# Issuing eight small w_phi loads between two transposed weight loads, on the sync queue of a TensorE-bound kernel

## The chip, the core and the metric

One Trainium2 chip, one of its cores. The metric is the device time of one execution in microseconds (us); lower is better.

## The reference

Two blocks read the same input `x` (1 x 2048 x 512, bf16) and are mixed by a sigmoid gate. Block A is linear attention with a feature map: each of 32 heads multiplies its 16-wide query and key by its own 16 x 16 matrix `w_phi` before two softmaxes. Block B is a gMLP with a 2048 x 2048 spatial matrix `w_sp`.

```python
qkv = (x @ wqkv).reshape(B, S, 3, 32, 16) ...           # q, k, v
pq  = einsum('bhsd,hdf->bhsf', q, w_phi)                # the same w_phi for q and k
pk  = einsum('bhsd,hdf->bhsf', k, w_phi)
phi = concat([softmax(p), softmax(-p)])                 # for q and for k
... kv, z, num / den, @ wo                              # a
z   = gelu(x @ w_in);  z2 = layernorm(z[..., 688:])
b   = (z[..., :688] * (w_sp @ z2 + b_sp)) @ w_out
out = g * a + (1 - g) * b                               # g = sigmoid(x . gate_w)
```

## The kernel before

Since `q @ w_phi` is `x @ (W_q @ w_phi)`, the kernel folds `w_phi` into the query and key weights once: `fold(1)` (the key fold) and `fold(0)` (the query fold). Each is 64 small matmuls that read a transposed copy of the weight (`wqkT`) and a block-diagonal copy of `w_phi` (`wphi`). Filling that copy takes eight small loads, one for each place of a head within a block of 128 rows.

All these loads are issued by the sync engine (SP), in program order, from one queue:

```python
    nc.sync.dma_start(out=brow[0:NT, :], in_=B_b_sp.rearrange("(t p) -> t p", p=P))
    for qk in (1, 0):                                   # key, then query, transposed
        nc.sync.dma_start_transpose(
            out=wqkT[:, qk * NDT:(qk + 1) * NDT, :], in_=A_wqkv[:, qk * D:(qk + 1) * D])
    heads = A_w_phi.rearrange("(kc u) e f -> u e kc f", u=8)
    for u in range(8):                                  # the eight small loads
        us = slice(u * DH, (u + 1) * DH)
        nc.sync.dma_start(out=wphi[us, :, us], in_=heads[u])
    for h in range(2):
        nc.sync.dma_start(out=wv_sb[:, 2 * h:2 * h + 2, :], in_=...)      # w_v
    for q in range(NCH):                                # four slabs of w_sp, transposed
        nc.sync.dma_start_transpose(
            out=wspT[:, :, q * CH:(q + 1) * CH], in_=B_w_sp[q * CH:(q + 1) * CH, :])
```

The program fixes the order of TensorE's instructions (in before's trace the folds come at 26.00 and 36.04 us). The folds stand in the middle of the first stage, behind the second z2 tile of the third and fourth block of rows:

```python
        for c in range(NCH):
            ts = list(range(c * 4, c * 4 + 4))
            for tt in ts:
                if c > 0:
                    z2_tile(tt)                         # 8 matmuls on line 191
                if c >= 2 and tt % 4 == 1:
                    later = fold(3 - c)                 # c=2: key, c=3: query; line 307
            ...                                         # z1 tiles, layernorm
```

A load is thus late only if it lands after TensorE has worked through the matmuls ahead of its fold.

The softmax here doesn't subtract the row's maximum and nothing guards it: scores larger than these inputs give would overflow.

Of the kernel before, what the change touches and what calls it, by code (L numbers as in the profile page):

```python
# [18 lines left out]
DH = 16  # L19
# [16 lines left out]
def kernel(  # L36
# [14 lines left out]
    nc = tc.nc  # L51
# [20 lines left out]
    wphi = early.tile([P, NDT, P], BF16, name="wphi")  # L72
# [32 lines left out]
        out=ramp[:, 0, :], data0=ones32[:, :], data1=zeros[:, :], initial=0.0,  # L105
# [4 lines left out]
    for q in range(4):  # L110
        qs = slice(32 * q, 32 * q + 32)
        nc.vector.tensor_tensor(
            out=ident[qs, qs], in0=ramp[qs, 0, :], in1=ramp[qs, 1, :], op=ALU.is_equal)
    nc.gpsimd.memset(brow[:], 0.0)
    nc.gpsimd.memset(wphi[:], 0.0)
    def load_z2w(eng, dt):
# [11 lines left out]
        out=scrap[:, :], in_=nc.const_aps.tensor(1.0, [P, 1], BF16), func=AF.Gelu_apprx_tanh)  # L128
# [5 lines left out]
    for h in range(2):  # L134
        nc.sync.dma_start(
            out=w_z1[:, 2 * h:2 * h + 2, :], in_=w_in_v[:, 2 * h:2 * h + 2, 0:FH])
    for i in range(4, 8):
        x_dma_T(i)
    for q in range(2, NCH):
        nc.sync.dma_start_transpose(  # L140
            out=xT[:, :, q * CH:(q + 1) * CH], in_=x2[q * CH:(q + 1) * CH, :]
        )
    nc.sync.dma_start(out=brow[0:NT, :], in_=B_b_sp.rearrange("(t p) -> t p", p=P))
    for qk in (1, 0):
        nc.sync.dma_start_transpose(
            out=wqkT[:, qk * NDT:(qk + 1) * NDT, :], in_=A_wqkv[:, qk * D:(qk + 1) * D])
    heads = A_w_phi.rearrange("(kc u) e f -> u e kc f", u=8)
    for u in range(8):
        us = slice(u * DH, (u + 1) * DH)
        nc.sync.dma_start(out=wphi[us, :, us], in_=heads[u])  # L150
    for h in range(2):
        nc.sync.dma_start(
            out=wv_sb[:, 2 * h:2 * h + 2, :],
            in_=A_wqkv[h * 2 * P:(h + 1) * 2 * P, 2 * D:3 * D].rearrange("(dt p) n -> p dt n", p=P),
        )
    for q in range(NCH):
        nc.sync.dma_start_transpose(
            out=wspT[:, :, q * CH:(q + 1) * CH], in_=B_w_sp[q * CH:(q + 1) * CH, :]
# [4 lines left out]
        out=mask4[:], in_=mask4[:], pattern=[[-32, NG]],  # L163
# [3 lines left out]
        out=mask4[:], in_=mask4[:], pattern=[[32, NG]],  # L167
# [3 lines left out]
        out=mask64[:, :, :], in_=mask4[:, :, None].to_broadcast([P, NG, DH]))  # L171
# [472 lines left out]
```

## Time and profile before

| | before |
|---|---|
| time, median of the first 3 runs | 206.76 us (206.36 to 206.82) |
| span in the profile | 204.5 us |
| TensorE busy | 200.8 us (98%) |
| granted TensorE clock (share of full speed), mean | 1.000 |
| key fold's operands read from | 25.9 us |
| query fold's operands read from | 36.0 us |

The page of before: the span; busy time, share of the span and instruction count of each engine (PE is TensorE); and the chain of waits, by engine and by line.

```profile
span 204.5 us, 3996 instructions
...
PE 200.8 (98%) x1557; PEld 119.9 (59%) x1557; DVE 130.4 (64%) x283; ACT 74.8 (37%) x122; POOL 45.6 (22%) x76
...
PE 98%; DVE 0%; issue 0%
PE mm L454 37%; PE zp L191 18%; PE mm L355 14%; PE mm L515 9%; PE mm L509 7%; PE mm L395 7%; PE kvacc L411 2%; PE at L467 2%; PE zp L222 1%; PE mm L520 1%; PE zp L307 0%; PE pq L280 0%; PE at L478 0%; PE pq L307 0%; DVE ob L527 0%; PE zp L230 0%
```

TensorE's own list of waits (what it waited for: us in all, times, longest):

```profile
engine line waited for: us in total, times, longest us
PE zp L222 <- PEq L628: 0.8, 1, 0.8
```

98% of the chain that ended last is TensorE, and TensorE waits for nothing after its first matmul. Line 191 is the first stage, line 454 the spatial matmul. A change that only moves loads can save at most what TensorE waits for loads, and here that list has no load in it.

The timeline of the SP queue (start, us, what was issued, out<-in, count). Durations are the time that SP spent issuing, not the transfer (the two transposes below took 2.43 and 2.30 us to issue and landed 5.2 to 5.5 us after their start):

```profile
15.37 4.78 SPq L145 DMA_TRANSPOSE wqkT<-in_A_wqkv_dram  x2
20.25 4.13 SPq L150 DMA_DIRECT2D wphi<-in_A_w_phi_dram  x8
24.43 0.94 SPq L152 DMA_DIRECT2D wv_sb<-in_A_wqkv_dram  x2
25.41 36.83 SPq L157 DMA_TRANSPOSE wspT<-in_B_w_sp_dram  x4
```

The key and query transposes take 4.78 us to issue together, the eight w_phi loads 4.13 us. The last w_phi load is issued at about 24.0 us (0.42 us ahead of the end of its row) and lands 1.6 us later at the earliest: at about 25.6.

The instructions of line 307, the folds. The first row gives the semaphore events of the weight loader's queue, the rest the loader's idle time by cause:

```profile
L307 PEldq EVENT_SEMAPHORE  x2: 51/51/51, 24.5 to 25.6; - x2
its engine sat idle before it (us, times) until:
  issue: 0.6, 2
```

The chain from 22 to 38 us (start, us, what; the many rows of 0.02 us inside the folds are left out):

```profile
23.64 2.36 PE zp L191 x16
26.00 0.12 PE zp L307 x2
...
26.58 9.45 PE zp L191 x64
36.04 0.12 PE zp L307 x2
...
36.75 1.27 PE zp L191 x8
```

The matmuls ahead of the key fold end at 26.00 us. The fold takes until 26.58 (0.58 us), 64 matmuls of line 191 until 36.04, the query fold until 36.75 (0.71 us). The second event, at 25.6, is the last w_phi load. So w_phi came 0.4 us ahead of its use: close, but in time.

### The profile page before, as it was taken

How to read it: one execution, taken by the hardware profiler on the slowest of the kernel's cores; microseconds unless marked ns; L12 is line 12 of the kernel's file. 1: busy time of each engine (PE TensorE's matmuls, PEld its weight loads, DVE VectorE, ACT ScalarE, POOL GpSimd, SP SyncE). 2: the span in 40 equal slices, each digit the busy share in tenths (PEclk: the TensorE clock that was granted, in tenths of full speed). 3: DMA queues.
4: the chain of work that ended last, by engine and by line, in shares of the span. 5: the costliest groups of instructions: out<-in, count | busy, mean ns of one | idle time of the engine just before them, and what ended most of it. 6: DMA issues, size and time to landing. Idle time of an engine off the chain costs nothing.

```text
span 204.5 us, 3996 instructions
## 1 busy us (share of the span) xinstructions
PE 200.8 (98%) x1557; PEld 119.9 (59%) x1557; DVE 130.4 (64%) x283; ACT 74.8 (37%) x122; POOL 45.6 (22%) x76
## 2 busy tenths in 40 slices
PE   8999999999999999999999999999999999999994
PEld 4666666655665555656565666555555555665642
DVE  4567484837977587979797789555566645633332
ACT  3566678796222333332424042222251136002303
POOL 3020202021523325334242442222204220200000
PEclk9999999999999999999999999999999999999999
DMA  6999699999999027940423219853567458552833
GB/s 194 252 205 171 80 151 290 146 278 247 256 249 213 3 38 182 287 94 16 75 48 45 51 38 120 154 109 64 105 161 80 90 113 183 63 96 51 156 64 104
DMA packets 89931, 27.22 MB, mean 133 GB/s; under 512 B 84184, under 2 KB 89912, under 8 KB 89912
## 3 DMA queue, kind: packets, MB, share of 16 engines
q1 hardware_dynamic: 87744, 24.99, 65.4%
q10 hardware_dynamic: 2168, 1.98, 3.5%
q8 instruction: 12, 0.20, 0.4%
q14 instruction: 7, 0.06, 0.1%
HBM read 4.15 MB, written 2.10 MB: 31 GB/s over the span
## 4 chain that ended last, share of the span: by engine, by line
PE 98%; DVE 0%; issue 0%
PE mm L454 37%; PE zp L191 18%; PE mm L355 14%; PE mm L515 9%; PE mm L509 7%; PE mm L395 7%; PE kvacc L411 2%; PE at L467 2%; PE zp L222 1%; PE mm L520 1%; PE zp L307 0%; PE pq L280 0%; PE at L478 0%; PE pq L307 0%; DVE ob L527 0%; PE zp L230 0%
## 5 line engine op out<-in xcount | busy, mean ns | idle before, releaser
L454 PE MATMUL mm<-z2all,wspT 128*128 128x344 bf16 x512 | 79.9, 309 | 0.0
L454 PEld LDWEIGHTS <-wspT 128*128 128x128 bf16 x512 | 49.0, 98 | 25.3
L191 PE MATMUL zp<-w_z,xT 128*128 128x344 bf16 (+1 forms) x254 | 38.1, 310 | 0.0
L359 ACT ACTIVATE eq<-mm 128x512 bf16<-128x512 f32 x32 | 17.4, 594 | 51.4 <-PE mm L355 25.7
L363 DVE TENSOR_REDUCE zs<-eq 128x64 f32<-128x1024 bf16 x16 | 19.5, 1220 | 20.0 <-ACT eq L359 20.0
L191 PEld LDWEIGHTS <-xT 128*128 128x128 bf16 x254 | 24.4, 98 | 11.8
L359 ACT ACTIVATE ek<-mm 128x512 bf16<-128x512 f32 x32 | 17.3, 600 | 27.1 <-PE mm L355 27.1
L459 DVE SCALAR_TENSOR_TENSOR ucat<-mm,bT,z1all 128x344 bf16<-128x344 f32 x32 | 17.4, 544 | 15.0 <-PE mm L454 15.0
L372 POOL TENSOR_TENSOR eq<-eq,ratio 128x512 bf16<-128x512 bf16 x16 | 16.9, 1055 | 44.6 <-DVE ratio L371 36.7
L531 ACT ACTIVATE ob<-mm,g_inv 128x512 bf16<-128x512 f32 (+1 forms) x15 | 10.1, 680 | 33.1 <-PE mm L520 28.5
L363 DVE TENSOR_REDUCE zs<-ek 128x64 f32<-128x1024 bf16 x16 | 19.3, 1209 | 2.8 <-ACT ek L359 2.8
L515 PE MATMUL mm<-wspT,uT 128*128 128x512 bf16 (+2 forms) x85 | 20.1, 367 | 0.0
L355 PEld LDWEIGHTS <-xT 128*128 128x128 bf16 x128 | 12.2, 98 | 12.0
L372 POOL TENSOR_TENSOR ek<-ek,ratio 128x512 bf16<-128x512 bf16 x16 | 16.9, 1056 | 2.2 <-DVE ratio L371 1.7
L509 PE MATMUL mm<-wspT,oT 128*128 128x512 bf16 (+2 forms) x68 | 16.6, 366 | 0.0
L355 PE MATMUL mm<-wq_p,xT 128*128 128x512 bf16 x64 | 16.4, 379 | 0.0
L395 PE MATMUL mm<-wv_sb,xT 128*128 128x512 bf16 x64 | 16.4, 379 | 0.0
L355 PE MATMUL mm<-wk_p,xT 128*128 128x512 bf16 x64 | 16.3, 379 | 0.0
L209 DVE BATCH_NORM_STATS2 bn<-z2all 128x6 f32<-128x344 bf16 x32 | 14.9, 501 | 0.0
L206 ACT ACTIVATE z2all<-zp 128x688 bf16<-128x688 f32 x16 | 11.8, 744 | 7.3 <-PE zp L191 7.2
L260 ACT ACTIVATE z1all<-zp 128x688 bf16<-128x688 f32 x16 | 11.9, 744 | 5.1 <-PE zp L191 4.6
L515 PEld LDWEIGHTS <-uT 128*128 128x128 bf16 x85 | 8.1, 98 | 9.4 <-issue 0.2
(77 smaller groups left out, 142.7 us busy)
## 6 DMA issues: line engine op xcount, KB each, us to landing
out_dram<-ob ACTq DMA_DIRECT2D x12, 128.0 KB, 2.4
wspT<-in_B_w_out_dram SPq DMA_DIRECT2D x2, 640.0 KB, 4.9
w_z<-in_B_w_in_dram SPq DMA_DIRECT2D x2, 344.0 KB, 4.7
w_z<-in_B_w_in_dram SPq DMA_DIRECT2D x3, 172.0 KB, 3.5
wv_sb<-in_A_wqkv_dram SPq DMA_DIRECT2D x2, 256.0 KB, 2.7
wspT<-in_A_wo_dram SPq DMA_DIRECT2D x2, 256.0 KB, 4.0
out_dram<-ob SPq DMA_DIRECT2D x3, 128.0 KB, 1.8
uT<-ucat SPq DMA_TRANSPOSE x16, 2.8
```

Of the source, the lines that this page charges most:

```text
L191: nc.tensor.matmul(zp[:, j, 0:n], lhsT=xT[:, dt, tt * P:(tt + 1) * P], rhs=wt[:, dt, j * HF:j * HF + n], start=(dt == 0), stop=(dt == NDT ...
L209: nc.vector.bn_stats(out=bn6[:, tt, j, :], in_=z2v[:, j, :])
L260: nc.scalar.activation(out=z1all[:, tt, :].rearrange("p (j n) -> p j n", j=2), in_=zp[:, :, 0:HF], func=AF.Gelu_apprx_tanh,)
L355: nc.tensor.matmul(ps[:, :], lhsT=xT[:, dt, tt * P:(tt + 1) * P], rhs=w[:, dt, :], start=(dt == 0), stop=(dt == NDT - 1))
L359: nc.scalar.activation(out=e[:, :, a, :], in_=ps[:, :].rearrange("p (h f) -> p h f", f=DH), func=AF.Exp, scale=1.0 - 2.0 * a)
L363: nc.vector.tensor_reduce(out=z[:].rearrange("p h a -> p (h a)"), in_=e[:].rearrange("p h a f -> p (h a) f"), axis=AX.X, op=ALU.add,)
L372: nc.gpsimd.tensor_tensor(out=e[:, :, 1, :], in0=e[:, :, 1, :], in1=ratio[:, :, None].to_broadcast([P, H, DH]), op=ALU.mult)
L395: nc.tensor.matmul(v_ps[:, :], lhsT=xT[:, dt, tt * P:(tt + 1) * P], rhs=wv_sb[:, dt, :], start=(dt == 0), stop=(dt == NDT - 1))
L454: nc.tensor.matmul(gp[:, 0:HF], lhsT=wspT[:, st, tt * P:(tt + 1) * P], rhs=z2all[:, st, j * HF:(j + 1) * HF], start=(st == 0), stop=(st == ...
L459: nc.vector.scalar_tensor_tensor(out=ucat[tt % NU][:, c0 + j * HF:c0 + (j + 1) * HF], in0=gp[:, 0:HF], scalar=bT[:, tt:tt + 1], in1=z1all[ ...
L509: nc.tensor.matmul(acc, lhsT=oTs[tt][:, g, :], rhs=wo_t[:, g, c0:c1], start=start and g == 0, stop=stop and g == NG - 1)
L515: nc.tensor.matmul(acc, lhsT=uTs[tt][:, i + ft, :], rhs=w_main[i][:, ft, c0:c1], start=start and ft == 0, stop=False)
```

## The change

The intent is to have w_phi in place early. The key fold needs it together with the key weights, ten microseconds before anything needs the query weights, yet it is issued behind the query transpose. The change swaps the two.

```diff
+    heads = A_w_phi.rearrange("(kc u) e f -> u e kc f", u=8)
     for qk in (1, 0):
         nc.sync.dma_start_transpose(
             out=wqkT[:, qk * NDT:(qk + 1) * NDT, :], in_=A_wqkv[:, qk * D:(qk + 1) * D])
-    heads = A_w_phi.rearrange("(kc u) e f -> u e kc f", u=8)
-    for u in range(8):
-        us = slice(u * DH, (u + 1) * DH)
-        nc.sync.dma_start(out=wphi[us, :, us], in_=heads[u])
+        for u in range(8 if qk == 1 else 0):
+            us = slice(u * DH, (u + 1) * DH)
+            nc.sync.dma_start(out=wphi[us, :, us], in_=heads[u])
```

The order of instructions on TensorE, VectorE, ScalarE and GpSimd is the same in both kernels; only SP's order changes, and with it some semaphore numbers.

## The prediction

> **What bounds the kernel now.** TensorE. On the page PE is busy 200.8 of 204.5 us (98%), the chain of waits is 98% PE, and PE's waits total 0.8 us, before the first matmul. The granted clock is 1.000. In the table by stretches PE is busy for the whole of each stretch from 15 to 75 us. So a load can cost time if it comes late, but can hardly give any back.
>
> **What the change does.** The same DMAs on the same SP queue; the order of instructions on PE, DVE, ACT and POOL is unchanged. Only the queue's order from 15 to 25 us moves. In before's timeline of SP:
> - key transpose issued 15.4 to 17.8 us, query transpose 17.85 to 20.15 (5.2 to 5.5 us from issue to landing);
> - eight w_phi loads 20.25 to 24.4 us (0.42 us each, 0.75 for one; landing after 1.6 to 3.3 us), the last issued at 24.0, so landing at about 25.6;
> - w_v from 24.4, four w_sp transposes from 25.4.
>
> PE reads w_phi and the key weights in the key fold at 25.9 us; the query fold is at 36.0; w_v is read at 45.6; w_sp at 46.3.
>
> So the last w_phi load lands only about 0.3 us ahead of the key fold: its semaphore event on the weight loader is at 25.6 us, and the weight loader idles 0.28 us. That is what the change aims at: w_phi 2.4 us earlier. But the matmuls queued ahead run until 26.0, so PE itself does not stand still; and the query fold, whose operands landed long before, starts with about the same weight-loader idle and the same 0.12 us step in the chain. That idle belongs to the fold's start, not to the load. Gain on the critical path: 0 to 0.15 us.
>
> **What it costs.** The query transpose is issued about 4.2 us later, at about 22, and should land at about 27.3, 8.7 us before its fold. The lane waits move too (a load waits for the DMA eight before it): the last w_phi load now waits for the key transpose, landed at about 20.7, when it is due at about 21.5; the query transpose waits for the first w_phi load. Neither should hold the queue by over 0.5 us. w_v should start within 0.5 us of 24.4, w_sp of 25.4; the first w_sp slab lands 12.9 us later, at 38.3, 8 us before its use. All this is slack. [...]I expect no new serialisation from alternating them.
>
> **Prediction.** 206.7 us, 80% range 206.1 to 207.3 (before: 206.36 to 206.82). Faster by over 2%: 0.01; within 2%: 0.98; slower by over 2%: 0.01.
>
> **What would show each step.** Right: PE busy about 200.8 and span about 204.5; key fold at 25.9 and query fold at 36.0, within 0.1 us; last w_phi issue at about 21.6, landing before 24; query transpose issued at about 22, landing by 28; w_sp from 25 to 26 us; the 0.28 us of weight-loader idle still there. Wrong: that idle gone and the fold earlier (the load was the wait); any PE wait at the query fold; w_sp over 1 us later.
>
> **What would make it wrong.** Unprofiled executions in which w_phi comes late, a cost that the profile hides (gain up to 1 us); a transpose that waits for all earlier plain loads, pushing the query transpose past 36 us; a shift of the later transposes of u and q on the same queue.

What is left of that sentence is my expectation alone ("them" are transposes and plain loads).

## The result, and the profile after

| | before | after |
|---|---|---|
| median of 6 runs | 206.66 us (206.23 to 206.82) | 206.22 us (206.05 to 206.73) |
| ratio, 95% interval | | 0.9987 (0.9971 to 1.0002) |
| span in the profile | 204.5 us | 204.5 us |
| TensorE busy | 200.8 us | 200.6 us |
| last w_phi issued | 24.0 us | 21.3 us |
| query transpose issued | 17.85 us | 21.79 us |

A ratio is the mean time of one kernel's runs over that of the other's of the same rounds, so it is not quite the ratio of the medians quoted. Executions over 1.5% slower than the fastest of the same kernel are left out of the means. The result is the same within 2%, and the interval includes one.

The page of after:

```profile
span 204.5 us, 3996 instructions
...
PE 200.6 (98%) x1557; PEld 119.5 (58%) x1557; DVE 130.5 (64%) x283; ACT 74.6 (36%) x122; POOL 45.8 (22%) x76
...
PE 95%; DMA 2%; SPq 1%; DVE 0%; issue 0%
```

TensorE's waits in after:

```profile
PE zp L222 <- PEq L628: 0.8, 1, 0.8
PE zp L191 <- DMA xT<-in_A_x_dram: 0.3, 1, 0.3
```

The 2% of DMA in the chain and the new 0.3 us wait belong to the first transposed load of `x`, at 7 us, long before the moved loads: the chain is followed back through that wait, so the matmuls ahead of it no longer count. The change cannot have caused it, and the profile of the same text run again (below) has no such wait.

The SP queue in after:

```profile
15.33 2.51 SPq L146 DMA_TRANSPOSE wqkT<-in_A_wqkv_dram  x1
17.94 3.81 SPq L150 DMA_DIRECT2D wphi<-in_A_w_phi_dram  x8
21.79 1.30 SPq L146 DMA_TRANSPOSE wqkT<-in_A_wqkv_dram  x1
23.14 1.22 SPq L152 DMA_DIRECT2D wv_sb<-in_A_wqkv_dram  x2
24.40 37.03 SPq L157 DMA_TRANSPOSE wspT<-in_B_w_sp_dram  x4
```

The eight w_phi loads begin at 17.94 us instead of 20.25, and the query transpose comes 3.9 us later. Something else was not foreseen: this transpose took 1.30 us to issue instead of 2.30, so that w_v and w_sp are issued about a microsecond *earlier* than before (24.40 against 25.41 us for w_sp).

The folds in after, and the chain of the same stretch:

```profile
L307 PEldq EVENT_SEMAPHORE  x2: 51/51/51, 24.6 to 24.8; - x2
...
  issue: 0.6, 2
```

```profile
23.81 2.36 PE zp L191 x16
26.16 0.12 PE zp L307 x2
...
26.75 9.45 PE zp L191 x64
36.20 0.12 PE zp L307 x2
...
36.79 1.28 PE zp L191 x8
```

The key fold takes 0.59 us and its start still has the same 0.28 us of loader idle (0.6 us over the two folds): that idle was never the load's. TensorE starts the fold 0.16 us later than in before; the wait at 7 us lies on that path. But the query fold takes 0.59 us here instead of 0.71, so that at the first matmul behind it, 36.79 against 36.75 us, most of the difference is gone. From that matmul to the copy of the last output tile (201.72 us in before, 201.76 in after) both profiles take 164.97 us, to the hundredth.

### The profile page after: what moved, and what is told of

Its sections match the earlier page's. It is cut to its first block, busy times and chain, and to the rows that moved or that the text cites. A ratio compares the mean times of both kernels' runs of the same rounds, so it can differ in the third digit from the quotient of the medians.

```text
span 204.5 us, 3996 instructions
## 1 busy us (share of the span) xinstructions
PE 200.6 (98%) x1557; PEld 119.5 (58%) x1557; DVE 130.5 (64%) x283; ACT 74.6 (36%) x122; POOL 45.8 (22%) x76
## 4 chain that ended last, share of the span: by engine, by line
PE 95%; DMA 2%; SPq 1%; DVE 0%; issue 0%
PE mm L454 37%; PE zp L191 17%; PE mm L355 14%; PE mm L515 8%; PE mm L509 7%; PE mm L395 7%; DMA xT<-in_A_x_dram 2%; PE kvacc L411 2%; PE at L467 2%; PE mm L520 1%; SPq L117 1%; PE zp L307 0%; PE at L478 0%; SPq L119 0%; PE pq L307 0%; DVE ob L527 0%
## 5 line engine op out<-in xcount | busy, mean ns | idle before, releaser
L454 PEld LDWEIGHTS <-wspT 128*128 128x128 bf16 x512 | 49.0, 98 | 25.3
L191 PEld LDWEIGHTS <-xT 128*128 128x128 bf16 x254 | 24.3, 98 | 12.4 <-DMA xT<-in_A_x_dram 0.6
```

What stands on the lines that cost most here:

```text
L191: nc.tensor.matmul(zp[:, j, 0:n], lhsT=xT[:, dt, tt * P:(tt + 1) * P], rhs=wt[:, dt, j * HF:j * HF + n], start=(dt == 0), stop=(dt == NDT ...
L454: nc.tensor.matmul(gp[:, 0:HF], lhsT=wspT[:, st, tt * P:(tt + 1) * P], rhs=z2all[:, st, j * HF:(j + 1) * HF], start=(st == 0), stop=(st == ...
```

## The experiments

**Two theories.** Mine: w_phi is in time in the old order, or so nearly that only tenths can be won, and the 0.4 us between the medians is spread. The rival: in executions that the one profile does not show, w_phi came late, and the new order saves it. Out of the chain views comes a measure far finer than the times: *the stretch*, from the end of the matmuls ahead of the key fold to the first matmul behind the query fold. It is free of what happens at the start and after the folds. The table has all 13 profiles. (The experiments ran on two chips; each ratio is to runs of before in the same rounds, on the same chip.) "Event" is the last of the weight loader's semaphore events at the key fold, "ready" the end of the matmuls ahead of it, "behind" the first matmul behind the query fold, and "rest" goes from there to the copy of the last output tile.

| profile | event | ready | behind | stretch | rest | span |
|---|---|---|---|---|---|---|
| *old order* | | | | | | |
| before | 25.6 | 26.00 | 36.75 | 10.75 | 164.97 | 204.5 |
| same_text | 26.1 | 25.92 | 36.96 | 11.04 | 164.97 | 204.7 |
| before_again | 25.4 | 26.74 | 37.37 | 10.63 | 164.97 | 205.1 |
| pad_2 | 26.1 | 26.31 | 36.93 | 10.62 | 164.98 | 204.8 |
| pad_4 | 26.8 | 26.50 | 37.60 | 11.10 | 164.97 | 205.6 |
| *w_phi earlier* | | | | | | |
| after | 24.8 | 26.16 | 36.79 | 10.63 | 164.97 | 204.5 |
| after_again | 24.7 | 26.05 | 36.68 | 10.63 | 164.97 | 204.4 |
| after_third | 25.3 | 26.73 | 37.36 | 10.63 | 164.97 | 205.1 |
| after_x_earlier | 25.3 | 26.71 | 37.34 | 10.63 | 164.97 | 205.1 |
| wphi_first | 25.1 | 26.50 | 37.12 | 10.62 | 164.97 | 204.9 |
| *w_phi or query later* | | | | | | |
| wphi_after_wv | 25.9 | 26.82 | 37.44 | 10.62 | 164.98 | 205.2 |
| query_after_slab | 25.3 | 26.71 | 37.88 | 11.17 | 164.97 | 205.6 |
| wphi_after_slab | 35.9 | 26.09 | 49.02 | 22.93 | 164.97 | 216.8 |

Where w_phi is early, the event comes 1.4 us ahead of "ready": that is merely when the loader's queue gets there. Where the gap is smaller, the load set it.

### The old text and the new text again, five rounds each

Edit of the first: none, the text of before. Edit of the second: none, the text of after.

> The kernel before, unchanged: a measure of what a ratio near one is worth. All theories: ratio 1.000, within 0.2%. If it comes out as far from one as the changed kernel's 0.9987, that 0.9987 is no sign of a gain.

> The changed kernel again, against before in 5 rounds on this chip. My theory (w_phi was never waited for by TensorE; the 0.4 us between the two medians is spread): ratio 0.999 to 1.001, spans overlapping those of before, TensorE's wait list without w_phi. Rival (executions in which w_phi came late cost the old order a few tenths): 0.998 to 0.999 again, with an interval below one. In either case w_sp should again start about 1 us earlier than before (24.4 against 25.4 us).

| | median | before beside it | ratio | 95% interval |
|---|---|---|---|---|
| same_text | 206.32 us | 206.41 us | 0.9990 | 0.9976 to 1.0004 |
| after_again | 206.21 us | 206.41 us | 0.9992 | 0.9976 to 1.0007 |

The unchanged text came out 0.9990 of itself. So neither 0.9987 nor 0.9992 is a sign of a gain, or against one: five rounds do not resolve 0.2 us. In the new text's profile w_phi is not among TensorE's waits. That alone proves little: the list of same_text has the same single row, `PE zp L222 <- PEq L628: 0.8, 1, 0.8`, and yet w_phi was late there, as shown next. In the new text w_sp was issued at 25.18 us, earlier than in the profile of same_text beside it (25.88), but not at the 24.4 us that I wrote.

The profile of same_text, however, goes against the strict form of my theory. Its queue, its folds and its chain:

```profile
15.40 5.46 SPq L145 DMA_TRANSPOSE wqkT<-in_A_wqkv_dram  x2
20.96 3.89 SPq L150 DMA_DIRECT2D wphi<-in_A_w_phi_dram  x8
```

```profile
L307 PEldq EVENT_SEMAPHORE  x2: 51/51/51, 24.4 to 26.1; - x2
...
  issue: 0.5, 2
  DMA wphi<-in_A_w_phi_dram: 0.3, 1
```

```profile
23.56 2.35 PE zp L191 x16
25.92 0.12 PE zp L307 x2
...
26.04 0.12 issue
...
26.79 9.45 PE zp L191 x64
36.24 0.12 PE zp L307 x2
...
36.96 1.13 PE zp L191 x7
```

Here the two transposes took 5.46 us to issue instead of 4.78, the last w_phi event came at 26.1 us, and TensorE was ready at 25.92. The key fold took 0.87 us (25.92 to 26.79) instead of 0.58. The loader's row for w_phi is no proof by itself, being as long as the 0.28 us of idle before every fold. But the trace has the fold stopping after its first matmuls and going on at 26.16 us, 0.13 us after the last w_phi load landed at 26.03; in pad_4 and wphi_after_slab (below), where w_phi was made late, that lag is 0.14 us. The wait that the change was meant to remove exists: 0.28 us, in this one execution of the unchanged text.

### A third profile of each

> A third profile of before's text, for the stretch from the end of the matmuls ahead of the key fold to the first matmul after the query fold. It was 10.75 and 11.04 us in the two profiles of that text, and 10.62 to 10.63 us in the four profiles whose w_phi was in time. My theory: the last w_phi event comes between 25.0 and 26.2 us, depending on how long the two weight transposes took to issue (4.1 to 5.5 us so far), and the stretch is 10.62 us where it comes ahead of 25.9 and up to 0.4 us longer where not. Rival (the order itself adds a fixed cost to the folds): at least 0.12 us longer whatever the landing time.

> A third profile of the changed text. Both theories: stretch 10.62 to 10.63 us, last w_phi landed over 2 us ahead of the key fold, the stretch from there to the last output store equal to the other profiles' 164.97 us. Any other value of the last would mean that the change reaches stages after the folds.

Edits: none. One execution each, 206.82 us both (state unknown, as with every single run). The old text's queue this time:

```profile
15.39 4.44 SPq L145 DMA_TRANSPOSE wqkT<-in_A_wqkv_dram  x2
19.92 4.05 SPq L150 DMA_DIRECT2D wphi<-in_A_w_phi_dram  x8
```

4.44 us of issue, event at 25.4, ready at 26.74, stretch 10.63 us: no loss at all. The fixed cost that the rival of this run expected is ruled out, and the new text gave 10.63 us for the third time. The mean of the three old profiles is (10.75 + 11.04 + 10.63) / 3 = 10.81 us, 0.18 us above the new text's 10.63: 0.09% of the time, well within all intervals above. Only about half of it can be put down to the order: of these three profiles one has lost time at the key fold (0.28 us, in the mean 0.09). The rest is 0.12 us in before and 0.13 in same_text, in the query fold (0.71 and 0.72 instead of 0.59 us), whose operands had long landed. The trace has it as one pause of 0.13 us between two of the fold's last matmuls (36.44 to 36.57 us in before). The three other profiles that the table calls old order (before_again, pad_2, pad_4) lack it. Its cause stays open.

### w_phi first of all

> The eight w_phi loads ahead of both weight transposes: w_phi even earlier (issued from about 15.4 to 19.2 us), both transposes about 3.8 us later, the key weights landing at about 24 us, ahead of the key fold at 26. My theory: ratio 0.999 to 1.001. Rival (earlier w_phi is worth something): at least the gain of the changed kernel, 0.998 to 0.999. If the query transpose's issue takes 2.3 us again here, where it follows directly on the key transpose, and not the 1.3 us of the changed kernel, then that saving is one of issuing behind a drained queue.

```diff
+    for u in range(8): ... nc.sync.dma_start(out=wphi[us, :, us], in_=heads[u])
     for qk in (1, 0): ... nc.sync.dma_start_transpose(out=wqkT[...], ...)
-    for u in range(8): ... nc.sync.dma_start(out=wphi[us, :, us], in_=heads[u])
```

206.36 us, ratio 0.9996 (0.9980 to 1.0012), stretch 10.62 us. More lead than the changed kernel gives is worth nothing. The query transpose, directly behind the key transpose again, took 2.13 us to issue, near the 2.3 us that I had named and not 1.30. I took that for a sign that the 1.30 us come from a drained queue. The record speaks against it as the whole reason: here the key transpose came directly behind the eight small loads, with the DMA engines as idle (share 0.08 from 19 to 19.6 us, against 0.10 in after and 1.42 in before from 20 to 22 us), and took 1.86 us. Over the profiles, the query transpose took 1.30 or 1.31 us to issue behind the eight small loads in after, after_again and after_third, but 2.04 us behind them in after_x_earlier, and 1.7 to 2.3 us directly behind the key transpose. What sets the issue time stays open.

### Later w_phi, three doses

> The eight w_phi loads behind the two w_v loads: w_phi 0.9 to 1.0 us later than before, the last one issued at about 24.9 and landing at about 26.6 us, behind the 26.0 us at which the queued matmuls end. My theory (before, w_phi landed 0.3 to 0.4 us ahead of its use): TensorE stands 0.6 to 0.9 us at the key fold, and the span grows by as much, so a ratio of 1.003 to 1.005. Rival (w_phi already is the wait in the order of before): the whole 1.0 us and more shows, 1.005 or above. A kernel bounded elsewhere would show nothing: 1.000.

```diff
-    for u in range(8): ... wphi ...
     for h in range(2): ... wv_sb ...
+    for u in range(8): ... wphi ...
```

206.86 us, ratio 1.0020 (1.0005 to 1.0036), but for another reason than expected: a miss. The transposes took only 4.17 us to issue this time, so that the last w_phi was issued at 24.2 and not 24.9 us; and TensorE was ready as late as 26.82, having started slowly. The event, at 25.9, was in time, and the stretch is 10.62 us. The 0.7 us between this span and before's come from that slow start (0.8 us later at "ready"), which lies ahead of the first moved load, and not from the folds. What slowed the start is read from the trace under "What is left of the spread". Why the six runs together are 0.2% slower is not settled by one profile.

The other way to delay w_phi is to put loads that nobody reads ahead of it:

> Before's order with two more small loads (2 KB each, into a tile that nobody reads) ahead of the eight w_phi loads, so that w_phi comes two issues (2 x 0.47 us) later. The two profiles of before's text had the last w_phi landing at 25.6 and 26.1 us, against key folds ready at 26.0 and 25.9, and lost 0 and 0.28 us there. My theory now (the order of before stands right at the edge, and each further delay is paid in full by TensorE): landing at 26.6 to 27.0 us, a wait at the key fold of 0.5 to 1.2 us, ratio 1.003 to 1.006. Rival (w_phi has slack of over a microsecond, the wait seen once is chance): no wait at the key fold, ratio 1.000.

> The same with four more small loads, w_phi 1.9 us later than in before. My theory: landing at 27.5 to 28.0 us, a wait of 1.5 to 2.1 us, ratio 1.007 to 1.010, that is 0.9 us on top of the two-load version. Rival: less than half a microsecond in all.

```diff
-    for u in range(8):
-        us = slice(u * DH, (u + 1) * DH)
-        nc.sync.dma_start(out=wphi[us, :, us], in_=heads[u])
+    for u in range(-4, 8):                              # -2 in pad_2
+        us = slice(max(u, 0) * DH, (max(u, 0) + 1) * DH)
+        nc.sync.dma_start(out=wphi[us, :, us] if u >= 0 else pad[:, u + 4], in_=heads[max(u, 0)])
```

pad_2: 206.84 us, ratio 1.0008 (0.9981 to 1.0035): nothing that can be told from zero; its profile had the event at 26.1, ready at 26.31, stretch 10.62 us. I had expected 0.5 to 1.2 us. The transposes issued quickly again (4.22 us), so that the last w_phi went out at 24.3 us, between before (24.0) and same_text (24.4). This profile is as the rival had it, while the interval of the runs still holds the 1.003 at the lower end of what I expected. pad_4: a median of 207.42 us in three runs, ratio 1.0060 (1.0023 to 1.0096; a fourth run, 210.67 us, counts as slow). Its chain now runs through the load:

```profile
25.20 1.59 DMA wphi<-in_A_w_phi_dram
26.79 0.14 issue
26.93 0.17 PE pq L307
```

The last w_phi load was issued at 25.20, landed at 26.79, and the fold went on from 26.93; TensorE had been ready at 26.50. The stretch is 11.10 us, 0.48 over the 10.62 us of a stretch without waits: less than the expected 1.5 to 2.1 in this execution, while the ratio is worth 1.2 us (0.0060 of 206.6). The direction is as I said, the size is not: what I left out of these two sums is that the issue time of the transposes ahead varies by over a microsecond (4.12 to 5.46 us in the seven profiles that issue key, query, and only then the rest), as much as the doses.

### A large dose

> The eight w_phi loads behind w_v and the first w_sp transpose: issued from about 31 to 35 us, landing at about 37 to 38 us behind that slab's data. My theory: TensorE stands at the key fold from 26 us until then, 11 to 12 us, and gets none of it back, since it has no idle time later: span 216, ratio 1.05 to 1.06. If later stages had hidden slack that could absorb it, under 1.04.

```diff
-    for u in range(8): ... wphi ...
     for h in range(2): ... wv_sb ...
     for q in range(NCH):
         nc.sync.dma_start_transpose(out=wspT[...], ...)
+        for u in range(8 if q == 0 else 0): ... wphi ...
```

217.42 us, ratio 1.0527 (1.0485 to 1.0569), worth 10.9 us; the profiled run is the slowest of the four (218.47 us). TensorE's waits at the first matmuls of the key fold (another row has 1.7 us more for the same loads):

```profile
PE zp L307 <- DMA wphi<-in_A_w_phi_dram: 7.7, 2, 7.2
```

From 26.09 us the key fold lasts until 36.69, that is 10.60 instead of 0.58 us: 10.02 us of waiting, a little under the 11 to 12 us expected. But the stretch grew by 12.30 us (22.93 - 10.63). The other 2.3 us are in this table by stretches (busy us and instruction count of each engine, then the granted clock, the DMA share and GB/s):

```profile
core 0: us, PE busy (x) PEld busy (x) DVE busy (x) ACT busy (x) POOL busy (x), PEclk, DMA share, GB/s
...
30.00:31.00 1.00, 0.00 (x0) 0.00 (x0) 0.00 (x0) 0.00 (x0) 0.00 (x0) 1.00 1.27 290
31.00:32.00 1.00, 0.00 (x0) 0.00 (x0) 0.00 (x0) 0.00 (x0) 0.00 (x0) 0.54 1.27 290
...
41.00:42.00 1.00, 1.00 (x8) 0.60 (x7) 0.16 (x1) 0.56 (x1) 0.00 (x0) 0.84 0.08 10
```

The granted clock falls to half at 31.1 us (0.54 between 31 and 32) and is back at 41.3 (0.84 between 41 and 42): 5.0 us after the last matmul ahead of the fold, and 5.3 us after TensorE was busy again at 36.0. With the granted clock at 0.50 until 41.3 us, the 64 matmuls of line 191 between the folds took 11.74 us instead of 9.45, and the end of the query fold comes 12.33 us after that of the key fold instead of 10.04 (in after). The 5.0 and 5.3 us are those of this one execution; what sets them was not measured. I had not expected the clock at all: that the time lands in the expected range is in part luck. From 49.02 us on nothing is gained or lost: the rest is 164.97 us again. So here the 10.02 us of waiting at the fold were paid in full, and 2.3 us on top of them.

### The query transpose's slack

> The changed order, but with the query transpose moved on behind the first w_sp transpose: issued at about 33 us instead of 22, landing at 37.5 to 38.5 us. The prediction said that the query transpose had about 8.7 us of slack after the change. My theory: 10 to 11 us of delay overruns that slack, and TensorE waits 1.5 to 2.5 us at the query fold, ratio 1.006 to 1.012; the key fold does not wait. If it shows nothing, the slack was larger than I said; if it shows over 4 us, smaller.

```diff
-    for qk in (1, 0): ... wqkT[key], wqkT[query] ...
+    ... wqkT[key] ...
     for u in range(8): ... wphi ...
     for h in range(2): ... wv_sb ...
     for q in range(NCH):
         nc.sync.dma_start_transpose(out=wspT[...], ...)
+        if q == 0: ... wqkT[query] ...
```

208.66 us, ratio 1.0099 (1.0050 to 1.0148), within the expected range of ratios. The profile, of the fastest of the four runs (207.34 us), has the query transpose issued at 31.50 and landed at 37.18 us, a wait of 0.5 us at the query fold (I had expected 1.5 to 2.5), none at the key fold, and a stretch of 11.17 us. That is 0.54 us more for a transpose issued 9.7 us later than in after. In after it was issued at 21.79 and landed 4.5 us later, at 26.3, 9.9 us ahead of its fold at 36.20; here its transfer took 5.7 us, which used up the rest. The three other runs lost more (spans 206.9 to 208.1 us), and no profile of theirs says where.

### What is left of the spread

> The changed order, and the fourth slice of the z2 weights issued from the scalar queue, so that the first transposed load of x is issued 0.47 us earlier (2.2 instead of 2.67 us). In the profile of the changed kernel TensorE waited 0.3 us for that load at 7 us, and the profiles differ from one another almost only ahead of 24 us. My theory (what is left of the spread comes from the first loads, not from w_phi): that wait is gone, ratio to before 0.997 to 1.000. Rival (the start is set by other loads or by the matmul clock): no difference from the changed kernel, 0.999.

```diff
-    load_z2w(nc.sync, 3)
+    load_z2w(nc.scalar, 3)
```

This on top of the changed order: 206.78 us, ratio 1.0004 (0.9990 to 1.0018), outside what I expected. No gain, and so no version that beats the two kernels. The wait for the first transposed load of `x` is gone, although that load, issued at 2.18 instead of 2.67 us, landed later than in after (7.77 against 7.23 us). Another wait stands in its place, among TensorE's waits:

```profile
PE zp L191 <- DMA w_z<-in_B_w_in_dram: 0.2, 1, 0.2
```

A slice of the z2 weights issued at 1.72 us landed 4.9 us later, at 6.6, where the median of such slices was 3.6 us in after. The load that was moved to the other engine landed no sooner either (6.78 against 6.17 us). Why is not shown by this single profile. The same row, for an earlier slice at 4.7 us, also stands in after_third, wphi_after_wv and wphi_after_slab, which have these first loads in the old order.

The loads are only one part of the start. The other goes with TensorE's clock. One matmul of the first stage, the same instruction each time, from TensorE's timeline (start, us, what) in before and then in before_again:

```profile
5.31 0.31 PE L230 MATMUL zp<-w_z,xT 128*128 128x344 bf16 x1
5.84 0.49 PE L230 MATMUL zp<-w_z,xT 128*128 128x344 bf16 x1
```

In before_again, pad_4 and wphi_after_wv the starts of such matmuls are 0.29 us apart at first and then 0.145: half the pace, then full. In before, whose clock record begins at 4.92 us, the first such matmul (at 4.53 us) took 0.44 us; in after, whose record begins at 3.76, the same one (at 4.42 us) took 0.31. In pad_4 and wphi_after_wv the step comes where the trace's clock record begins, with full clock, at 6.08 and 6.40 us; in same_text the record begins at 4.67 us. (Ahead of its first entry the views show a granted clock of 1.00 for want of a record.) "Ready" follows: 25.92 us in same_text, 26.00 in before, 26.50 in pad_4, 26.82 in wphi_after_wv, the last with 0.2 us of waiting for a load besides. From before to pad_4, half of the 1.16 us is 0.58 (an estimate), and "ready" differs by 0.50. After's earlier record (3.76 us) did not help it: the wait of 0.3 us for `x` took that lead away. All this lies ahead of 8 us, and the first moved load is issued at 15.

So the table shows where the spread of the spans sits: "ready" goes from 25.92 to 26.82 us, whatever the order of w_phi, with the moment of full clock and with the waits for the first loads; no run changes one of the two alone. Each profile without a wait at the folds has a span of 178.3 to 178.5 us beyond its "ready".

## Why the prediction was right

The measured 206.22 us lies in the range of 206.1 to 207.3, near its lower end, and the class (within 2%) was right. Both are a weak test: "within 2%" had been given 0.98, and the 0.44 us between the two medians, which put the result near that end, is little more than the old text's own medians differ by (206.32 to 206.66 us). Point by point:

- *TensorE is the bound, and a load that comes earlier gives nothing back.* Shown by the rest of 164.97 or 164.98 us in every profile and by wphi_first (stretch 10.62 us).
- *The 0.28 us of loader idle is the fold's own.* Shown: it is there in after too, with w_phi early.
- *Gain 0 to 0.15 us.* Right in number for the profiled execution, but by luck: the 0.12 us lie in the pause of the query fold, where no gain was argued. Too small as a general statement: old-order stretches of 10.63, 10.75 and 11.04 us against 10.63 give 0, 0.12 and 0.41 us. What I named as a risk, executions in which w_phi comes late, was real at 0.28 us in one profile of three.
- *The query transpose has about 8.7 us of slack.* It had 9.9 us in after, and query_after_slab, 9.7 us later, just overran it (0.54 us).
- *No new serialisation from alternating transposes and plain loads* (my expectation). This trace shows none: the query transpose is issued at 21.79 us, 0.04 us after the last w_phi issue ends. Nor did the "lane waits" hold the queue. In this program's trace each of these loads waits for, and raises, one of eight semaphores in turn, that of the load eight before it: in after the last w_phi load has the semaphore of the key transpose (103), the query transpose that of the first w_phi load (104). The last seven w_phi loads took 0.42 us each.
- *w_v within 0.5 us of 24.4, w_sp from 25 to 26.* Wrong in the profile of after: 23.14 and 24.40 us, because the query transpose issued in 1.30 instead of 2.3 us. Harmless, since both have slack.
- *Key fold at 25.9 and query fold at 36.0 us, within 0.1.* They came at 26.1 and 36.2, moved by what happened ahead of 8 us. A position in absolute time was the wrong check; the stretch between two of TensorE's own marks is the right one.

What the times alone cannot say is whether there is a gain. The profiles show one where w_phi came late, 0.28 us in one of three; the medians of the unchanged text differ by up to 0.34 us, and its single executions by 0.9.

## What to carry to other kernels

On a kernel whose bounding engine has no waits, moving loads is insurance, not speed (here a ratio of 0.9987, 0.9971 to 1.0002): ask how far ahead of its use each load lands, how much the issue times ahead of it vary, and whether the slack covers that; here 0.4 us of slack stood against over a microsecond of variation, and the swap gave it 2.6 us more from slack that another load had to spare. To measure an effect below the spread of the times, compare a stretch between two marks on the bounding engine over several profiles, and run the unchanged text beside the changed one. Do not rely on TensorE's list of waits alone: a wait inside a fold stood in the chain and in the landing times, and not in that list. Small doses on a queue of varying issue times tell little; one large dose told that lateness was paid in full (10.02 us), and that this much waiting cost another 2.3 us through a granted clock of 0.50.
